# Pooled attention into a gated conv FFN: the depthwise conv of two and a half sequences moved from TensorE to ScalarE and VectorE, late pooling moved to GpSimd

## The chip, the cores and the metric

One NeuronCore of a Trainium2 chip runs the whole kernel in one launch. The metric is the device time of one execution in microseconds (us); lower is better. A difference of about 0.5% (1.1 us here) is what a measurement of this kernel can tell from no change.

## The reference

```
# attention, per sequence b (8) and head h (8), S = 576, D = 64
k_p, v_p = mean of k, v over 8 neighbouring positions     # 72 positions
attn = softmax(q @ k_p.T / 8)                             # 576 x 72
x[b] = concat over heads of attn @ v_p                    # 576 x 512
# gated FFN
h    = relu(x @ w_in)                                     # 576 x 1024
conv = w[0]*h[s-1] + w[1]*h[s] + w[2]*h[s+1]              # per channel, along the sequence
out  = (h * sigmoid(conv)) @ w_out                        # 576 x 512
```

q, k, v and the output are float32 in device memory; inside the kernel all operands of TensorE are bf16.

## The kernel before

**Sequences and groups.** The eight sequences are handled in four groups of two (0,1), (2,3), (4,5), (6,7). The order in which sequences reach the FFN is 0, 1, 3, 2, 4, 5, 6, 7. The attention of a group is cut into nine or ten row tiles of up to 128 rows; the FFN of a sequence into eight blocks `fb` of 128 of the 1024 channels; the output of a group into nine row tiles.

**Loads.** GpSimd (POOL) issues all loads of q, k, v and of the two weight matrices (L260 to L296), and they are converted to bf16 on the way. Keys of sequences 2 to 7 come in pairs into the only `kk` buffer (L267); v has three buffers (L278, L281).

**Pooling.** Keys of a pair are summed over 8 positions by three halving adds, `pool_pair` (L411: 2304, 1152, 576 elements for each partition), v by three halving adds and a masked product, `prep_v` (L457: 1280, 640, 320 elements; L461: 960). All of these run on VectorE (DVE). The keys are turned by TensorE (PE) into `kT` (L417, L440).

**Attention of a row tile.** Scores (PE, L553 or L566), row maximum (DVE, L579), subtraction of it (DVE L591, or for group 0 PE L599), exp (ScalarE, ACT, L617), a turn of the result (PE L628 with a copy L642, or from group 2 on a DMA, L637), the product with the pooled v (PE, L653), division by the row sum (DVE, L666 and L668), and a turn into `xT` (PE L685 and copy L693, or a DMA, L677).

**FFN of a sequence.** For each `fb`, two halves of `ffn_in` (PE, L698, four matmuls of 288 columns each; for sequence 0 by row tiles, L719) and a relu into `hT` (ACT, L707). The conv runs on PE as products with diagonal matrices `dw`. Sequences 0 to 3 do it in 64x64 tiles of the array (`ffn_conv`, L832), sequences 4 to 7 in 32x32 tiles (`ffn_conv16`, L790): one set of 48 matmuls covers four `fb` (an index `f4`, 0 or 1) and half a sequence, so a sequence takes four sets. `hT` has 64 more columns at each end; for sequences 4 to 7 GpSimd fills these by two copies for each `f4` (`ffn_wrap`, L780 and L781), so that a shifted tap is one plain slice. ACT takes tanh of the conv out of PSUM (L800, L843), DVE makes the gate from it: add 1 (L815, L854, L857: `tensor_scalar`, bf16, SBUF to SBUF) and multiply with `hT` (L819, L861: `tensor_tensor`, both operands in SBUF). Since 32x32 tiles leave their results on other partitions than they belong on, `ffn_gate16` adds 1 in five or six pieces of 32 to 128 partitions for each pair of `fb`.

**Output.** `ffn_out` (PE, L869, eight matmuls of 512 columns for a row tile, in two halves `j`), a copy of PSUM into `osb` (DVE or ACT, L880), and the store from SP or ACT (L892).

**Order.** Nothing is scheduled at run time. `Graph.ORDER` lists every operation of the kernel by number, with the engine where there is a choice, `FORMS` and `PLACES` give the tile modes and the buffers, and every engine works its own part of that list strictly in order, waiting on semaphores. The costs in the `add(...)` calls were used by a planner that is no longer in the file.

Of the kernel before, what the change touches and what calls it, by code (L numbers as in the profile page):

```python
# [33 lines left out]
class Graph:  # L34
# [23 lines left out]
    Q_DMA = (3,)  # L58
    SHIFT_DVE = 1
# [52 lines left out]
    )  # L112
    FORMS = (
        0, 1, 0, 0, 1, 1, 1, 1, 1, 0, 0, 0, 0, 1, 0, 0, 0, 0, 0, 0, 1, 1, 1, 0, 0, 0, 1, 0, 1, 0, 0, 0, 1, 0, 1, 1, 0, 0, 0, 0,
    )
    PLACES = (
# [51 lines left out]
def kernel(  # L168
# [759 lines left out]
    def nudge(kind, b):  # L928
        return 0.0
# [367 lines left out]
```

## Time and profile before

| | |
|---|---|
| median of 3 runs | 227.65 us (226.90 to 228.12) |
| the profiled execution, its own time | 227.96 us |
| the span of its profile | 226.2 us |
| mean granted TensorE clock | 0.992 |

The span runs from the first to the last instruction of the program; 1.76 us of the execution's own time lie around it. In the profile PE is a matmul, DVE VectorE, ACT ScalarE, POOL GpSimd, SP SyncE. A matmul's duration includes its way through the array, and matmuls overlap: 512 columns are shown with 374 ns, but they start 216 ns apart. How much room PE has is therefore read from start to start, not from the busy share. In what follows a stage is named by the sequence whose `ffn_in` begins it; in the trace of before these begin at 59.05 (sequence 1), 77.91 (3), 107.77 (2), 122.24 (4), 141.24 (5), 166.59 (6) and 184.75 us (7).

### The profile page before, as it was taken

The numbers are of one execution on the slowest core, as the hardware profiler recorded it, in microseconds if no ns is written. First come the engines' busy times: TensorE is split into PE (matmuls) and PEld (weight loads), VectorE is DVE, ScalarE is ACT, GpSimd is POOL, SyncE is SP. The second block draws the span as 40 slices with busy tenths as digits, with TensorE's granted clock in tenths as the row PEclk, the third lists the DMA queues.
The fourth block names the chain that finished last, engine by engine and source line by source line (L and its number), as shares of the span: only waits on it lengthen the run. The fifth ranks groups of instructions, "written<-read, shape, count | busy, mean of one in ns | idle before, by whom it ended". The sixth has DMA issues, their size and how long they took to land.

```text
span 226.2 us, 8092 instructions
## 1 busy us (share of the span) xinstructions
PE 210.7 (93%) x3469; PEld 143.9 (64%) x3469; DVE 189.5 (84%) x410; ACT 142.0 (63%) x239; POOL 35.8 (16%) x65
## 2 busy tenths in 40 slices
PE   7587999969999999999999999999998999999991
PEld 3556699855788777665787844666466646644451
DVE  7588877999999999989999998899984896859631
ACT  2057657999998878685679734783644746564220
POOL 7944231023220120000000010012001310110000
PEclk9799999999999999999999999999999999999999
DMA  5999999999999899864664574676567445021585
GB/s 85 177 191 207 207 207 207 207 207 206 208 208 206 128 192 128 194 149 84 156 127 99 113 120 104 139 153 108 71 129 168 99 51 139 3 51 35 142 200 183
DMA packets 48840, 32.72 MB, mean 145 GB/s; under 512 B 28300, under 2 KB 44324, under 8 KB 48804
## 3 DMA queue, kind: packets, MB, share of 16 engines
q0 software_dynamic: 16288, 16.26, 44.2%
q1 hardware_dynamic: 31716, 14.77, 32.4%
q10 hardware_dynamic: 800, 1.18, 1.6%
q8 instruction: 27, 0.44, 0.8%
q14 instruction: 9, 0.07, 0.1%
HBM read 32.52 MB, written 9.44 MB: 185 GB/s over the span
## 4 chain that ended last, share of the span: by engine, by line
PE 68%; DVE 19%; issue 5%; ACT 4%; DMA 1%; DVEq 0%; ACTq 0%
PE psum L869 25%; PE psum L698 18%; PE psum L653 5%; PE psum L790 4%; PE psum L719 4%; PE psum L832 4%; DVE negm L579 3%; DVE sd L591 2%; ACT tg L843 2%; PE psum L566 2%; PE psum L628 2%; DVE gT L857 2%; DVE x L668 2%; DVE gT L815 1%; DVE gT L861 1%
## 5 line engine op out<-in xcount | busy, mean ns | idle before, releaser
L869 PE MATMUL psum<-w_out_sb,gT 128*128 128x512 bf16 (+1 forms) x296 | 69.4, 374 | 0.5 <-DVE gT L861 0.5
L698 PE MATMUL psum<-xT,w_in_sb 128*128 128x288 bf16 x448 | 63.3, 286 | 0.8 <-DVE sd L591 0.5
L698 PEld LDWEIGHTS <-w_in_sb 128*128 128x128 bf16 x448 | 41.8, 98 | 14.4 <-issue 1.9
L707 ACT ACTIVATE hT<-psum 128x576 bf16<-128x576 f32 x56 | 35.1, 651 | 23.4 <-PE psum L698 21.0
L869 PEld LDWEIGHTS <-gT 128*128 128x128 bf16 x296 | 26.8, 98 | 26.5 <-DVE gT L861 0.7
L815 DVE TENSOR_SCALAR gT<-tg 32x576 bf16<-32x576 bf16 (+2 forms) x88 | 27.0, 307 | 7.1 <-ACT tg L800 5.9
L579 DVE TENSOR_REDUCE negm<-psum 128x8 f32<-128x576 f32 (+2 forms) x37 | 27.6, 752 | 2.9 <-PE psum L566 1.6
L668 DVE TENSOR_TENSOR x<-psum,r 128x512 bf16<-128x512 f32 (+1 forms) x37 | 25.6, 691 | 1.3
L800 ACT ACTIVATE tg<-psum 128x576 bf16<-128x576 f32 x32 | 19.4, 648 | 8.6 <-PE psum L790 5.6
L880 ACT COPY osb<-psum 128x512 f32<-128x512 f32 x21 | 12.2, 590 | 14.9 <-PE psum L869 10.5
L843 ACT ACTIVATE tg<-psum 128x576 bf16<-128x576 f32 x32 | 19.5, 652 | 2.6 <-PE psum L832 1.9
L617 ACT ACTIVATE e<-sd 128x576 bf16<-128x576 f32 x27 | 18.4, 685 | 4.2 <-DVE sd L591 4.2
L591 DVE TENSOR_TENSOR sd<-psum,negm 128x576 f32<-128x576 f32 x27 | 20.2, 754 | 0.8
L780 POOL COPY hT<-hT 128x252 bf16<-128x252 bf16 x8 | 3.5, 438 | 108.4 <-ACT hT L707 108.4
L653 PE MATMUL psum<-vm,eT 128*128 128x65 bf16 (+5 forms) x240 | 18.5, 221 | 1.6 <-DMA eT<-e 1.0
L653 PEld LDWEIGHTS <-eT 128*128 128x128 bf16 (+1 forms) x240 | 15.1, 101 | 5.2 <-DMA eT<-e 1.2
L832 PE MATMUL psum<-hT,dw 64*64 64x288 bf16 (+2 forms) x512 | 15.8, 256 | 0.5 <-ACT hT L707 0.2
L880 DVE COPY osb<-psum 128x512 f32<-128x512 f32 (+1 forms) x16 | 10.5, 653 | 6.8 <-PE psum L869 6.7
L832 PEld LDWEIGHTS <-dw 64*64 64x64 bf16 x512 | 12.6, 107 | 3.7 <-issue 2.7
L457 DVE TENSOR_TENSOR v<-v 128x1280 bf16<-128x1280 bf16 (+2 forms) x24 | 13.0, 542 | 1.3 <-DMA v<-in_v_dram 1.2
L819 DVE TENSOR_TENSOR gT<-gT,hT 128x1152 bf16<-128x1152 bf16 x16 | 12.5, 778 | 0.6
L642 ACT COPY eT<-psum 128x640 bf16<-128x640 bf16 (+1 forms) x17 | 11.1, 666 | 2.9 <-PE psum L628 2.8
(83 smaller groups left out, 254.7 us busy)
## 6 DMA issues: line engine op xcount, KB each, us to landing
out_dram<-osb SPq DMA_DIRECT2D x62, 128.0 KB, 2.4
v<-in_v_dram POOLq DMA_DIRECT2D x8, 512.0 KB, 16.2
qp<-in_q_dram POOLq DMA_DIRECT2D x7, 576.0 KB, 13.8
kk<-in_k_dram POOLq DMA_DIRECT2D x3, 1152.0 KB, 16.9
w_in_sb<-in_moe_w_in_dram POOLq DMA_DIRECT2D x2, 512.0 KB, 16.9
w_out_sb<-in_moe_w_out_dram POOLq DMA_DIRECT2D x1, 1024.0 KB, 24.5
out_dram<-osb ACTq DMA_DIRECT2D x8, 128.0 KB, 3.0
kk<-in_k_dram POOLq DMA_DIRECT2D x2, 288.0 KB, 5.0
```

Of the source, the lines that this page charges most:

```text
L579: nc.vector.tensor_reduce(out=a["m"][0:rows], in_=a["s"][0:rows, :, 0:2 * KW].rearrange("p a (h s) -> p a h s", s=Sp), axis=AX.X, op=OP.ma ...
L591: nc.vector.tensor_tensor(out=a["d"][0:rows], in0=a["s"][0:rows, :, 0:2 * KW].rearrange("p a (h s) -> p a h s", s=Sp), in1=a["m"][0:rows]. ...
L653: nc.tensor.matmul(out=a["o"][lo:hi, h // 4, (h % 4) * (D + 1):(h % 4 + x1 - x0) * (D + 1)], lhsT=a["eT"][:, j, lo:hi], rhs=buf("vm", b)[: ...
L668: nc.vector.tensor_tensor(out=a["x"][0:rows].rearrange("p (a h d) -> p a h d", a=2, d=D), in0=ov[:, :, :, 0:D], in1=r[0:rows].unsqueeze(3) ...
L698: nc.tensor.matmul(out=banks(ps)[:, j, 0:SC], lhsT=w_in_block(dc, fb), rhs=buf("xT", g)[:, dc, i * S + j * SC:i * S + (j + 1) * SC], start ...
L707: nc.scalar.activation(out=h_of(b)[:, fb].rearrange("p (a s) -> p a s", a=2), in_=banks(ps)[:, :, 0:SC], func=ACT.Relu, scale=0.5,)
L800: nc.scalar.activation(out=buf("tg", b, f4, h)[:, :, j * SC:(j + 1) * SC], in_=banks(ps)[:, :, 0:SC], func=ACT.Tanh, scale=0.5,)
L815: nc.vector.tensor_scalar(out=gate[lo:lo + n, 4 * f4 + s], in0=tg[src:src + n, x], scalar1=1.0, scalar2=None, op0=OP.add)
L832: nc.tensor.matmul(out=banks(pss[r ^ c])[c * D:(c + 1) * D, j, lo:hi], lhsT=dw[r * D:(r + 1) * D, tap * n_fb + fb, :], rhs=hT[r * D:(r + 1 ...
L843: nc.scalar.activation(out=tg.rearrange("p (a s) -> p a s", a=2), in_=banks(ps)[:, :, 0:SC], func=ACT.Tanh, scale=0.5,)
L869: nc.tensor.matmul(out=bank(ps)[0:rows, columns], lhsT=buf("gT", g)[:, fb, t * P:t * P + rows], rhs=w_out_sb[:, fb, columns], start=(fb == 0),
L880: copy(out=osb[0:rows, columns], in_=bank(ps)[0:rows, columns])
```

## The change

- **Taps.** For both halves `f4` of sequences 5 and 6 and for `f4` 0 of sequence 7 the conv is no longer done by PE. For each `fb`: ACT writes `w[1]*h` in float32 (Identity, with the weight as a scale for each partition), DVE adds the two other taps (`scalar_tensor_tensor`, 576 elements, bf16 and float32 in, float32 out), ACT takes tanh of that and writes it straight into `gT`. For each `f4`, DVE then adds 1 and multiplies by `hT` in two instructions of 2304 elements.
- **Pooling.** `prep_v` of sequences 3 to 7 and `pool_pair` of groups 2 and 3 run on GpSimd.
- **`ffn_conv`** reads `hT` with its offset, and its shorter runs stand in another order; its columns are the same. `ffn_in` of a half waits only for the attention tiles of that half.
- **Order.** ORDER, FORMS and PLACES are written out anew for all engines. In the new list DVE takes 6 instead of 16 of the output copies, 6 instead of 2 of the `eT` copies, 6 instead of 3 of the `xT` copies and 7 instead of 5 of the `qT` copies; ACT takes the others.

```diff
+    WRAP = (4, 5, 6, 7)
+    TAPS = ((5, 0), (5, 1), (6, 0), (6, 1), (7, 0))
+    V_POOL = (3, 4, 5, 6, 7)
+    K_POOL = (2, 3)
...
     def pool_pair(g, step):
         t, half = buf("kk", g), POOL * D >> step + 1
-        nc.vector.tensor_tensor(out=t[:, :, 0:half], in0=t[:, :, 0:half], in1=t[:, :, half:2 * half], op=OP.add)
+        engine = nc.gpsimd if g in Graph.K_POOL else nc.vector
+        engine.tensor_tensor(out=t[:, :, 0:half], in0=t[:, :, 0:half], in1=t[:, :, half:2 * half], op=OP.add)
...
     def prep_v(b, step):
+        engine = nc.gpsimd if b in Graph.V_POOL else nc.vector
...
-    def conv_todo():
+    def conv_todo(wrapped):
+        if wrapped:
+            return [[(tap, 0, SC, tap * TB + j * SC) for tap in (1, 0, 2)] for j in range(2)]
...
-                todo[j].append((tap, lo - j * SC, hi - j * SC, src))
-        return todo
+                todo[j].append((tap, lo - j * SC, hi - j * SC, TB + src))
+        return [[t[0]] + sorted(t[1:], key=lambda x: (x[2] - x[1]) % SC) for t in todo]
...
+    def ffn_tap(b, fb, tap):
+        acc, w = buf("tg", b, fb // 4, "tap", fb), convw[:, tap * n_fb + fb:tap * n_fb + fb + 1]
+        acc = acc.rearrange("p a s -> p (a s)").bitcast(FP32)
+        h = buf("hT", b)[:, fb, tap * TB:tap * TB + S]
+        if tap == 1:
+            nc.scalar.activation(out=acc, in_=h, func=ACT.Identity, scale=w)
+        else:
+            nc.vector.scalar_tensor_tensor(out=acc, in0=h, scalar=w, in1=acc, op0=OP.mult, op1=OP.add)
+
+    def ffn_tap_tanh(b, fb):
...
+        nc.scalar.activation(out=buf("gT", g)[:, fb, i * S:(i + 1) * S], in_=acc, func=ACT.Tanh, scale=0.5)
+
+    def ffn_tap_gate(b, f4):
...
+        nc.vector.tensor_scalar(out=gate, in0=gate, scalar1=1.0, scalar2=None, op0=OP.add)
+        nc.vector.tensor_tensor(out=gate, in0=gate, in1=h_of(b)[:, four], op=OP.mult)
...
-            prev = add(dve(d), key + nudge("kk", g) + Graph.KPOOL + step, lambda step=step: pool_pair(g, step),
+            prev = add({"POOL": 0.1 + (5.0, 2.5, 1.25)[step]} if g in Graph.K_POOL else dve(d), key + nudge("kk", g) + Graph.KPOOL + step, lambda step=step: pool_pair(g, step),
...
-            prev = add(dve(d), key + step * gap, lambda step=step: prep_v(b, step),
+            prev = add({"POOL": 0.1 + (2.8, 1.4, 0.7, 2.1)[step]} if b in Graph.V_POOL else dve(d), key + step * gap, lambda step=step: prep_v(b, step),
...
+    def half_of(b, j):
+        g, i = where[b]
+        ts = (0, 1, 2, 3, 4) if i == 0 else (9 if g in Graph.APART else 4, 5, 6, 7, 8)
+        return [xdone[g, t] for t in (ts[2:] if j else ts[:3])]
...
-                            after=need + [win[fb // 4], o], uses=[big, xtok[g], htok[b]], mode=FULL, count=8)
+                            after=half_of(b, j) + [win[fb // 4], o], uses=[big, xtok[g], htok[b]], mode=FULL, count=8)
...
+        for f4 in range(n_fb // 4):
+            if (b, f4) not in Graph.TAPS:
+                continue
+            tanh = []
+            for fb in range(4 * f4, 4 * f4 + 4):
+                tg, o = token("tg", b, f4, "tap", fb), None
+                for tap in (1, 0, 2):
+                    o = add(act(0.667) if tap == 1 else dve(0.757), w, lambda fb=fb, tap=tap: ffn_tap(b, fb, tap),
+                            after=[wraps[f4], dw0, o], uses=[tg, htok[b]])
+                tanh.append(add(act(0.667), w, lambda fb=fb: ffn_tap_tanh(b, fb), after=[o], uses=[tg, gtok[g]]))
+            gated = add(dve(0.75, 1.36), w, lambda f4=f4: ffn_tap_gate(b, f4), after=tanh, uses=[htok[b], gtok[g]])
+            gdone.setdefault(b, []).append(gated)
         for f4 in range(n_fb // 4 if b in Graph.SIXTEEN else 0):
+            if (b, f4) in Graph.TAPS:
+                continue
```

More of the change, by code (lines that the diff above doesn't have):

```diff
@@ L62 @@
     ORDER = (
[49 rows of a table removed]
[51 rows of a table added]
     )
     FORMS = (
-        0, 1, 0, 0, 1, 1, 1, 1, 1, 0, 0, 0, 0, 1, 0, 0, 0, 0, 0, 0, 1, 1, 1, 0, 0, 0, 1, 0, 1, 0, 0, 0, 1, 0, 1, 1, 0, 0, 0, 0,
+        0, 1, 0, 0, 1, 1, 1, 1, 1, 0, 0, 0, 0, 1, 0, 0, 0, 0, 0, 0, 0, 1, 1, 0, 0, 0, 0, 0, 0, 0, 0, 1, 1, 1, 1, 1, 0, 0, 1, 0,
     )
     PLACES = (
[18 rows of a table removed]
[17 rows of a table added]
     )
@@ L456, in prep_v @@
             half = POOL * D >> step + 1
-            nc.vector.tensor_tensor(
+            engine.tensor_tensor(
                 out=vt[:, :, 0:half], in0=vt[:, :, 0:half], in1=vt[:, :, half:2 * half], op=OP.add
@@ L460, in prep_v @@
             return
-        nc.vector.tensor_tensor(
+        engine.tensor_tensor(
             out=buf("vm", b)[:, :, :, 0:D],
@@ L819, in ffn_gate16 @@
         nc.vector.tensor_tensor(out=gate[:, both], in0=gate[:, both], in1=h_of(b)[:, both], op=OP.mult)
+    def ffn_tap(b, fb, tap):
[8 more added lines that the diff above has]
+        g, i = where[b]
+        acc = buf("tg", b, fb // 4, "tap", fb).rearrange("p a s -> p (a s)").bitcast(FP32)
+        nc.scalar.activation(out=buf("gT", g)[:, fb, i * S:(i + 1) * S], in_=acc, func=ACT.Tanh, scale=0.5)
+    def ffn_tap_gate(b, f4):
+        g, i = where[b]
+        four = slice(4 * f4, 4 * f4 + 4)
+        gate = buf("gT", g)[:, four, i * S:(i + 1) * S]
+        nc.vector.tensor_scalar(out=gate, in0=gate, scalar1=1.0, scalar2=None, op0=OP.add)
+        nc.vector.tensor_tensor(out=gate, in0=gate, in1=h_of(b)[:, four], op=OP.mult)
     def ffn_conv(b, f2, pss):
-        hT, todo = h_of(b), conv_todo()
+        hT, todo = buf("hT", b), conv_todo(b in Graph.WRAP)
         for turn in range(2):
@@ L1154 @@
     hdone, gdone, htok, gtok = {}, {}, {}, {}
+    def half_of(b, j):
+        g, i = where[b]
+        ts = (0, 1, 2, 3, 4) if i == 0 else (9 if g in Graph.APART else 4, 5, 6, 7, 8)
+        return [xdone[g, t] for t in (ts[2:] if j else ts[:3])]
     def add_ffn(b, w):
@@ L1161, in add_ffn @@
             gtok[g] = token("gT", g)
-        need = [xdone[g, t] for t in (range(5) if i == 0 else range(5, 10) if g in Graph.APART else range(4, 9))]
         relu = {}
@@ L1181, in add_ffn @@
                     o = add(pe(*[SC] * 4), w + 3 * fb + nudge("i", 8 * b + fb), lambda fb=fb, j=j, big=big: ffn_in(b, fb, j, big),
-                            after=need + [win[fb // 4], o], uses=[big, xtok[g], htok[b]], mode=FULL, count=8)
+                            after=half_of(b, j) + [win[fb // 4], o], uses=[big, xtok[g], htok[b]], mode=FULL, count=8)
                 relu[fb] = [add(act(0.65), w + 3 * fb + nudge("i", 8 * b + fb), lambda fb=fb, big=big: ffn_relu(b, fb, big), after=[o],
                                 uses=[big, htok[b]])]
+        wraps = [add({"POOL": 0.8}, w, lambda f4=f4: ffn_wrap(b, f4), uses=[htok[b]],
+                     after=[o for fb in range(4 * f4, 4 * f4 + 4) for o in relu[fb]] + [ends])
+                 for f4 in range(n_fb // 4 if b in Graph.WRAP else 0)]
+        for f4 in range(n_fb // 4):
[10 more added lines that the diff above has]
+            gdone.setdefault(b, []).append(gated)
         for f4 in range(n_fb // 4 if b in Graph.SIXTEEN else 0):
+            if (b, f4) in Graph.TAPS:
+                continue
             tgs = [token("tg", b, f4, h) for h in range(2)]
             tanh = [[], []]
-            wrap = add({"POOL": 0.8}, w, lambda f4=f4: ffn_wrap(b, f4), uses=[htok[b]],
-                       after=[o for fb in range(4 * f4, 4 * f4 + 4) for o in relu[fb]] + [ends])
+            wrap = wraps[f4]
             for j in range(2):
@@ L1202, in add_ffn @@
             fbs = (2 * f2, 2 * f2 + 1)
+            if (b, f2 // 2) in Graph.TAPS:
+                continue
             cbs, tg = [token("ps", n=2) for _ in fbs], token("tg", b, f2 // 2, f2 % 2)
-            conv = add({"PE": 0.75}, w + 6 * f2 + Graph.QCONV + nudge("c", 4 * b + f2), lambda f2=f2, cbs=cbs: ffn_conv(b, f2, cbs),
-                       after=relu[fbs[0]] + relu[fbs[1]] + dwo, uses=cbs + [tg, htok[b], gtok[g]], mode=QUARTER, count=64)
+            conv = add({"PE": 0.64 if b in Graph.WRAP else 0.66}, w + 6 * f2 + Graph.QCONV + nudge("c", 4 * b + f2), lambda f2=f2, cbs=cbs: ffn_conv(b, f2, cbs),
+                       after=(wraps[f2 // 2:f2 // 2 + 1] or relu[fbs[0]] + relu[fbs[1]]) + dwo, uses=cbs + [tg, htok[b], gtok[g]],
+                       mode=QUARTER, count=48 if b in Graph.WRAP else 64)
             for fb, cb in zip(fbs, cbs):
```

135 rows, old and new, of tables (ORDER, PLACES) are left out of this document.

## The prediction, on record before the changed kernel ran

> **What bounds the kernel now.** I read the page first, then the busy time by stage (the stretch of the trace that each sequence's `ffn_in` begins), then single conv sets in the timeline. The page's share of busy time and its chain of what ended last:
>
> ```profile
> PE 210.7 (93%) x3469; PEld 143.9 (64%) x3469; DVE 189.5 (84%) x410; ACT 142.0 (63%) x239; POOL 35.8 (16%) x65
> PE 68%; DVE 19%; issue 5%; ACT 4%; DMA 1%; DVEq 0%; ACTq 0%
> ```
>
> The chain lies two thirds on PE and one fifth on DVE. The stages tell why DVE is there at all (columns: stretch, its length, then the busy time of each engine):
>
> ```profile
> core 0: us, PE busy (x) PEld busy (x) DVE busy (x) ACT busy (x) POOL busy (x), PEclk, DMA share, GB/s
> 59.05:77.91 18.86, 18.71 (x325) 15.12 (x324) 18.45 (x38) 17.47 (x34) 3.64 (x5) 1.00 1.13 186
> 77.91:107.77 29.86, 29.25 (x455) 19.91 (x447) 28.33 (x55) 22.01 (x38) 1.33 (x2) 1.00 0.83 149
> 141.24:166.59 25.35, 25.03 (x443) 15.60 (x442) 23.73 (x55) 15.39 (x27) 2.00 (x4) 1.00 0.63 117
> 166.59:184.75 18.16, 17.12 (x299) 11.00 (x298) 13.70 (x34) 10.32 (x18) 3.50 (x6) 1.00 0.64 123
> 184.75:226.20 41.45, 36.80 (x472) 20.02 (x472) 24.76 (x61) 16.51 (x28) 1.66 (x4) 1.00 0.39 103
> ```
>
> From 59 to 108 us PE and DVE are both full: DVE is busy 46.8 of 48.7 us. From 141 us on PE alone is full; DVE idles 1.6, 4.5 and 16.7 us in the three last stages, ACT 10.0, 7.8 and 24.9. GpSimd is nearly empty everywhere. So the change takes from PE where PE binds, gives to DVE and ACT where they have room, and takes pooling from DVE where DVE is as full as PE.
>
> **Term 1: PE loses ten conv sets.** Two lines of the timeline (start, length, what):
>
> ```profile
> 182.99 0.73 PE L790 MATMUL psum<-hT,dw 32*32 32x288 bf16 x48
> 183.65 1.04 PE L869 MATMUL psum<-w_out_sb,gT 128*128 128x512 bf16 x4
> ```
>
> A set holds PE for 183.65 - 182.99 = 0.66 us, the change of tile mode included. Sixteen sets become six: 10 x 0.66 = **-6.6 us**. Six of these go from the stages of sequences 4 to 6, four from the last. The matmuls of `ffn_conv` (sequences 0 to 3) keep their columns and change places only; I cost that, and the finer waits of `ffn_in` (each half on its own tiles, in a fixed order), at nothing. The loads at the head stand in another order too (the first half of `w_in` before q of sequence 2); as the same bytes come, also nothing, with 1.5 us to either side.
>
> **Term 2: what DVE and ACT take on at the end.** The groups by form (count | busy, mean ns | idle before):
>
> ```profile
> L815 DVE TENSOR_SCALAR gT<-tg 32x576 bf16<-32x576 bf16 x64 | 19.5, 304 | 0.9
> L815 DVE TENSOR_SCALAR gT<-tg 128x576 bf16<-128x576 bf16 x8 | 2.6, 328 | 2.6 <-ACT tg L800 2.6
> L819 DVE TENSOR_TENSOR gT<-gT,hT 128x1152 bf16<-128x1152 bf16 x16 | 12.5, 778 | 0.6
> L591 DVE TENSOR_TENSOR sd<-psum,negm 128x576 f32<-128x576 f32 x27 | 20.2, 754 | 0.8
> L411 DVE TENSOR_TENSOR kk<-kk 128x2304 bf16<-128x2304 bf16 x3 | 4.1, 1352 | 0.8 <-DMA qp<-in_q_dram 0.8
> L617 ACT ACTIVATE e<-sd 128x576 bf16<-128x576 f32 x27 | 18.4, 685 | 4.2 <-DVE sd L591 4.2
> L800 ACT ACTIVATE tg<-psum 128x576 bf16<-128x576 f32 x32 | 19.4, 648 | 8.6 <-PE psum L790 5.6
> L880 ACT COPY osb<-psum 128x512 f32<-128x512 f32 x21 | 12.2, 590 | 14.9 <-PE psum L869 10.5
> L880 DVE COPY osb<-psum 128x512 f32<-128x512 f32 x14 | 9.6, 686 | 6.2 <-PE psum L869 6.1
> ```
>
> For each of the five `f4`, DVE gives up eleven pieces of add 1 (304 ns) and two products (778): 4.9 us. It takes eight taps of 576 float32 elements; none is in the trace, the nearest row is L591 with 754 ns, the bounds are the bf16 add 1 of as many elements (0.33) and the 2304-element product (1.35). I take 0.754: 6.0 us. It takes one add 1 of 2304 elements (between 0.33 and four times that, 1.31; I take 0.8) and a product of 2304 (1.35 by L411). Together 8.2 - 4.9 = 3.3, five times: +16.3 us. Ten output copies leave it, -6.9. Net +9.4 us against 22.8 us of idle time, of which the time after the last gate (40 matmuls of 216 ns, about 9 us) doesn't count. ACT takes 20 first taps and 20 tanh from SBUF (685 each by L617, bounds 590 and 1.35 us) for 20 of L800, plus ten copies: 27.4 - 13.0 + 5.9 = +20.3 us into 42.7 us of idle time. Both fit, but in the middle stage (sequence 6) three engines are then full, and each tap is a round ACT, DVE, DVE, ACT with three `tg` buffers for it. After the last `ffn_in` the new order gives PE 16 half output tiles and two sets, 15 us, and DVE eight taps, a copy and three gates, 13.7 us, before five output tiles that need the last gate. I charge **+1.6 us**, a quarter of term 1; the bounds are 0 (the idle time takes all) and 6.6 (the taps set the end and nothing is won).
>
> *On ACT, "ScalarE: Activation LUTs" of the Trainium skill (What ACT_TABLE_LOAD costs) says that an operand read for each partition through a pointer adds about 93 ns to an ACTIVATE; no row here has such a scale. By it the 20 first taps would cost 1.9 us more on ACT, and the sum would be at most that much later.*
>
> **Term 3: pooling on GpSimd, and who waits for it.** In the two stages that PE and DVE fill, DVE is freed of these (L457, L411 and L461 in that stretch, each in its own answer; below them two copies that it takes):
>
> ```profile
> 59.05:107.77 48.72, 4.85 (x9) 1.00 0.95 163
> 59.05:107.77 48.72, 5.10 (x6) 1.00 0.95 163
> 59.05:107.77 48.72, 1.94 (x3) 1.00 0.95 163
> ...
> L642 DVE COPY eT<-psum 128x640 bf16<-128x640 bf16 x2 | 1.0, 488 | 0.4 <-PE psum L628 0.4
> L693 DVE COPY xT<-psum 128x512 bf16<-128x512 bf16 x2 | 0.8, 416 | 0.0
> ```
>
> That is 11.9 us. The new list gives DVE 3 `eT` copies, 5 `xT` copies and 2 output copies more in these stages, 1.5 + 2.1 + 1.4 = 4.9 us, so it has 46.8 - 11.9 + 4.9 = 39.8 us to do in 48.7: **8.9 us of slack**.
>
> What GpSimd does to DVE meanwhile is visible in before, at the small copies of `ffn_wrap`:
>
> ```profile
> 198.56 0.40 POOL L780 COPY hT<-hT 128x252 bf16<-128x252 bf16 x1 [3.75 <-ACT hT L707]
> 155.36 0.40 POOL L780 COPY hT<-hT 128x252 bf16<-128x252 bf16 x1 [6.85 <-ACT hT L707]
> 155.44 0.93 DVE L819 TENSOR_TENSOR gT<-gT,hT 128x1152 bf16<-128x1152 bf16 x1
> 155.70 0.93 POOL L781 COPY hT<-hT 128x252 bf16<-128x252 bf16 x1
> 193.84 0.30 DVE L815 TENSOR_SCALAR gT<-tg 32x576 bf16<-32x576 bf16 x1
> 193.89 0.51 POOL L780 COPY hT<-hT 128x252 bf16<-128x252 bf16 x1 [11.99 <-ACT hT L707]
> 194.15 0.41 DVE L815 TENSOR_SCALAR gT<-tg 32x576 bf16<-32x576 bf16 x1
> 194.35 0.47 POOL L781 COPY hT<-hT 128x252 bf16<-128x252 bf16 x1
> 194.57 0.40 DVE L815 TENSOR_SCALAR gT<-tg 32x576 bf16<-32x576 bf16 x1
> L304 POOL TENSOR_SCALAR_AFFINE_SELECT gT<-gT x2: 781/799/817, 5.7 to 6.5; 64x648 bf16<-64x648 bf16 x2
> ```
>
> A copy alone takes 0.40 us. At 155.4 the gate's product started while a copy ran and took 0.93 instead of 0.78; the next copy, started 0.26 us into that product, ended just after it, at 156.6. At 193.8 the two engines go strictly in turn, and each instruction is longer by what the other had left. So a gate's instructions and a GpSimd instruction on SBUF exclude each other, whole instruction by whole instruction. So far the partner took 0.4 us; now it takes microseconds.
>
> *"SBUF — State Buffer" of the Trainium skill (Who interferes with whom) has this as a rule: VectorE in a two-port mode or with two SBUF inputs and GpSimd share a port pair under an exclusive lock for a whole instruction. By that rule the trace agrees.*
>
> Price of a GpSimd instruction: the copy (252 elements, 0.40) and the select of L304 (648, 0.80) give 1.0 ns for each element and 0.15 us for one input. No row has two inputs; bounds are 1.0 ns (inputs read together) and 3.2 (twice the copy's whole 1.58 ns). I take twice the slope, 2.0 ns: `prep_v` 2.7, 1.4, 0.8, 2.1 us (7.0), `pool_pair` 4.75, 2.45, 1.3 (8.5).
>
> *"GPSIMD Engine Reference" of the Trainium skill (3.1) gives 2.6 cycles at 1.2 GHz for an element of a two-input operation, 2.17 ns; by that figure the stall below would be about 8% larger, some 1.3 us.*
>
> In the two stages the new list has 17 such instructions (three steps of sequence 3, sequences 4 and 5, both pairs): 35.3 us of 48.7, a share of 0.72. DVE has 13 gates there, seven of one port instruction (add 1) and six of three (two adds, a product). A first instruction meets a running GpSimd one with that share, and then waits for its rest, the sum of squares over twice the sum, 96/70.6 = 1.36 us: 13 x 0.72 x 1.36 = 12.7 us. Each of the twelve that follow inside a gate can let in one whole GpSimd instruction, 2.08 us on average: at most 12 x 0.72 x 2.08 = 18.0. As a longer stage thins GpSimd's share (0.60), and as GpSimd often waits for a landing or for a pair's single `kk` buffer, I take 10.6 of the first and a third of the second, 5.4: **16 us of stall on DVE**, bounds 5 (priced at 1.0 ns, first instructions alone) and 31. Behind a stalled gate stand the row maxima, subtractions and divisions of the attention, and PE waits for these. Less the slack: 16 - 8.9 = **+7.1 us**. DVE's row maxima, subtractions and divisions read PSUM and go untouched.
>
> GpSimd's queue is in order, and loads now stand behind pooling: the load of pair 3 behind pair 2's three adds, v of sequence 5 behind the first add of sequence 4, v of 6 and 7 behind parts of pair 3. Before, such loads waited too:
>
> ```profile
> POOL v L278 <- DVE vm L461: 16.5, 3, 7.2
> POOL kk L267 <- DVE negm L579: 7.8, 1, 7.8
> ```
>
> so I charge nothing for the loads; if the gates hold GpSimd up in turn (25 instructions, 7 x 0.33 + 12 x 0.30 + 6 x 0.78 = 10.6 us), the keys of pair 3 come late for their turn at the start of sequence 2, some us of PE that the upper bound holds.
>
> **Sum.** 227.96 (the profiled execution's own time) - 6.6 + 1.6 + 7.1 = 230.1 us. That execution was 0.31 us above the median, so **229.8 us** on the median's scale.
>
> **Rivals.** (1) *Not slower: the stalls fit into DVE's slack.* Place: the two stages from 59 to 108 us; it decides below 8.9 us of stall, for instance if GpSimd's adds cost 1.0 ns an element. Then 227.65 - 6.6 + 1.6 = 222.6 us; with the taps hidden too, 221.0. For it: 8.9 us is half of what I expect, and GpSimd idles while it waits for landings. Against it: the strict turns at 193.8. (2) *The port decides fully*: 31 us of stall, 227.65 - 5.0 + 22.1 = 244.8; halfway there, 237. For it: gates and pooling together want 10.6 + 35.3 = 46 of the port's 48.7 us. Against: GpSimd must be ready at each gate. (3) *They cancel*: stalls of 13 to 15 us, or taps that end last without stalls, both 227 to 228.7. That the change doesn't do what it says is hardly possible: the new list has 288 matmuls of L790's kind for 768.
>
> **How the numbers follow.** Forecast 0.45 (226.5 to 238 is its own range), rival 1 0.33, rival 2 0.12, rival 3 0.10. Slower by over 0.5% (about what a measurement of this kernel can tell from no change): 0.57; within: 0.10; faster: 0.33. The range must reach into rival 1 and half into rival 2: 221.5 to 239.0 leaves out the best of the one and the worst of the other.
>
> **What would show it.** Term 1: conv sets 16 to 6, PE's stages of sequences 5 and 7 shorter. Term 2: taps near 0.75 us, no DVE or ACT wait that ends in the last gate. Term 3: GpSimd adds of 2 to 5 us, and DVE's add-1 and product groups with means far above 304 to 328 and 778 ns between 59 and 115 us; the sum of that excess is the stall. If those means stay within 0.3 us of before, term 3 is wrong and rival 1 holds.

## The result and the profile after

The changed kernel takes **255.3 us** (median of 4 runs, 253.82 to 257.65) beside 227.4 us for the kernel before on the same chip (226.9 to 228.12): a ratio of 1.120, 95% interval 1.116 to 1.124. Here and below a median is of all runs, while a ratio leaves out runs that took over 1.5% longer than the fastest of their kernel (here the one of 257.65 us). That is slower, as forecast, but the loss is 27.9 us where the forecast had 2 and the top of the range 11. The profiled execution has a span of 252.7 us. Its page begins like this (busy time of each engine, then the chain that ended last):

```profile
PE 209.8 (83%) x2993; PEld 142.6 (56%) x2993; DVE 213.4 (84%) x368; ACT 154.7 (61%) x260; POOL 92.2 (36%) x91
...
PE 40%; DVE 34%; DMA 10%; issue 8%; POOL 4%; ACT 2%; DVEq 0%; ACTq 0%; POOLq 0%
```

DVE is busy 24 us longer than before, although it has been relieved of pooling, and its part of the chain rises from 19 to 34%. The busy time by stage (start and end, length, busy time of each engine, granted clock):

```profile
core 0: us, PE busy (x) PEld busy (x) DVE busy (x) ACT busy (x) POOL busy (x), PEclk, DMA share, GB/s
0.00:64.46 64.46, 50.91 (x972) 38.28 (x972) 54.20 (x114) 38.68 (x63) 29.30 (x45) 1.00 1.15 187
64.46:83.53 19.07, 18.74 (x305) 15.70 (x306) 16.39 (x32) 15.13 (x27) 10.71 (x6) 1.00 0.49 75
83.53:133.89 50.36, 33.64 (x452) 22.18 (x450) 44.30 (x51) 19.39 (x34) 27.90 (x18) 0.80 0.70 119
133.89:148.31 14.42, 14.26 (x285) 11.21 (x285) 13.52 (x29) 10.29 (x19) 0.00 (x0) 1.00 0.42 89
148.31:173.15 24.84, 20.26 (x321) 12.81 (x319) 19.96 (x39) 13.62 (x23) 11.62 (x9) 1.00 0.66 100
173.15:192.89 19.74, 19.12 (x258) 12.31 (x259) 17.72 (x38) 15.31 (x26) 3.36 (x6) 1.00 0.60 116
192.89:210.10 17.21, 16.49 (x121) 10.86 (x121) 17.00 (x26) 15.58 (x28) 3.53 (x3) 1.00 0.49 103
210.10:252.70 42.60, 36.35 (x289) 19.23 (x287) 30.29 (x46) 26.69 (x46) 5.81 (x6) 0.97 0.48 124
```

Against before, the head is 5.4 us longer (59.05 to 64.46), the stage of sequence 1 as long (18.86 to 19.07), that of **sequence 3 longer by 20.5** (29.86 to 50.36), that of 4 by 5.8 (19.00 to 24.84); those of 5 and 6 are shorter by 5.6 and 0.95, the last longer by 1.15. The stages of 4 and 5 are best read together: the one has 70 matmuls more than before (251 to 321), the other 185 less (443 to 258), and only 96 of these are conv sets that are gone from the two. Work has moved across their border, and the two together are as long as before (44.35 to 44.58). The stage of 3 alone holds three quarters of the loss. GpSimd is busy for 27.9 us in it, where it had 1.33.

The groups by form tell what changed there (count | busy, mean ns | idle before):

```profile
L837 DVE SCALAR_TENSOR_TENSOR tg<-hT,convw,tg 128x576 f32<-128x576 bf16 x40 | 31.0, 823 | 0.2
L887 DVE TENSOR_SCALAR gT<-tg 64x576 bf16<-64x576 bf16 x32 | 20.9, 654 | 0.6
L891 DVE TENSOR_TENSOR gT<-gT,hT 128x1152 bf16<-128x1152 bf16 x16 | 15.6, 978 | 0.6
L835 ACT ACTIVATE tg<-hT,convw 128x576 f32<-128x576 bf16 x20 | 15.1, 771 | 0.1
L842 ACT ACTIVATE gT<-tg 128x576 bf16<-128x576 f32 x20 | 13.2, 684 | 4.0 <-DVE tg L837 4.0
L464 POOL TENSOR_TENSOR v<-v 128x1280 bf16<-128x1280 bf16 x5 | 13.1, 2620 | 5.9 <-DMA v<-in_v_dram 5.9
L884 DVE TENSOR_SCALAR gT<-tg 128x576 bf16<-128x576 bf16 x16 | 11.3, 712 | 1.3 <-ACT tg L873 1.3
L417 POOL TENSOR_TENSOR kk<-kk 128x2304 bf16<-128x2304 bf16 x2 | 9.1, 4540 | 0.6 <-DMA kk<-in_k_dram 0.6
```

The gate's three groups (L884, L887, L891; L854, L857, L861 before) were 5.0, 9.9 and 12.1 us; they are 11.3, 20.9 and 15.6, 20.8 us more for the same instructions. The lines of GpSimd and DVE in the timeline from 81.7 to 88.3 us show how one add 1 of 0.31 us comes to last 3.5 us (start, length, engine, line; x2 is two instructions in one line):

```profile
81.72 1.01 POOL L272 DMA_DIRECT2D kk<-in_k_dram  x1 [8.14 <-PE psum L692]
82.05 6.19 DVE L887 TENSOR_SCALAR gT<-tg 64x576 bf16<-64x576 bf16 x2
82.74 2.62 POOL L464 TENSOR_TENSOR v<-v 128x1280 bf16<-128x1280 bf16 x1
85.30 0.79 POOL L283 DMA_DIRECT2D v<-in_v_dram  x1
86.08 0.56 POOL L286 DMA_DIRECT2D v<-in_v_dram  x1
86.66 2.26 POOL L464 TENSOR_TENSOR v<-v 128x640 bf16<-128x640 bf16 x2
88.27 1.27 DVE L891 TENSOR_TENSOR gT<-gT,hT 128x1152 bf16<-128x1152 bf16 x1
```

The first add 1 starts during the issue of a load, has not run when that issue ends, and then waits for the whole 2.62 us add of v; it ends just after it, at 85.5. The second meets the two issues of the next load and the first of the two adds behind them, and ends at 88.2. Two instructions of 0.31 us have taken 6.19.

### The profile page after: what moved, and what is told of

Read it like the earlier page. It is cut to its first block, busy times and chain, and to the rows that moved or that the text cites. A ratio compares the mean times of both kernels' runs of the same rounds, so it can differ in the third digit from the quotient of the medians.

```text
span 252.7 us, 7119 instructions
## 1 busy us (share of the span) xinstructions
PE 209.8 (83%) x2993; PEld 142.6 (56%) x2993; DVE 213.4 (84%) x368; ACT 154.7 (61%) x260; POOL 92.2 (36%) x91
## 4 chain that ended last, share of the span: by engine, by line
PE 40%; DVE 34%; DMA 10%; issue 8%; POOL 4%; ACT 2%; DVEq 0%; ACTq 0%; POOLq 0%
PE psum L705 13%; PE psum L899 12%; DVE tg L837 8%; DMA qp<-in_q_dram 7%; DVE gT L887 6%; DVE negm L586 4%; DVE sd L598 3%; PE psum L726 3%; DMA xT<-x 3%; PE psum L660 3%; PE psum L862 3%; DVE gT L891 2%; DVE gT L884 2%; DVE x L675 2%; DVE v L464 1%
## 5 line engine op out<-in xcount | busy, mean ns | idle before, releaser
L705 PE MATMUL psum<-xT,w_in_sb 128*128 128x288 bf16 x448 | 66.4, 295 | 13.8 <-DVE sd L598 7.7
L789 POOL COPY hT<-hT 128x252 bf16<-128x252 bf16 x8 | 6.7, 843 | 90.0 <-ACT hT L714 69.9
L837 DVE SCALAR_TENSOR_TENSOR tg<-hT,convw,tg 128x576 f32<-128x576 bf16 x40 | 31.0, 823 | 0.2
L873 ACT ACTIVATE tg<-psum 128x576 bf16<-128x576 f32 x32 | 19.2, 650 | 18.3 <-issue 12.9
L464 POOL TENSOR_TENSOR v<-v 128x1280 bf16<-128x1280 bf16 (+2 forms) x15 | 24.2, 1610 | 6.5 <-DMA v<-in_v_dram 5.9
L910 ACT COPY osb<-psum 128x512 f32<-128x512 f32 (+1 forms) x31 | 17.4, 579 | 11.9 <-PE psum L899 10.1
L887 DVE TENSOR_SCALAR gT<-tg 64x576 bf16<-64x576 bf16 x32 | 20.9, 654 | 0.6
L624 ACT ACTIVATE e<-sd 128x576 bf16<-128x576 f32 x27 | 18.1, 682 | 3.7 <-DVE sd L598 3.7
L417 POOL TENSOR_TENSOR kk<-kk 128x2304 bf16<-128x2304 bf16 (+2 forms) x6 | 16.5, 2754 | 0.7 <-DMA kk<-in_k_dram 0.6
L891 DVE TENSOR_TENSOR gT<-gT,hT 128x1152 bf16<-128x1152 bf16 x16 | 15.6, 978 | 0.6
L842 ACT ACTIVATE gT<-tg 128x576 bf16<-128x576 f32 x20 | 13.2, 684 | 4.0 <-DVE tg L837 4.0
```

The source lines that it names most:

```text
L464: engine.tensor_tensor(out=vt[:, :, 0:half], in0=vt[:, :, 0:half], in1=vt[:, :, half:2 * half], op=OP.add)
L705: nc.tensor.matmul(out=banks(ps)[:, j, 0:SC], lhsT=w_in_block(dc, fb), rhs=buf("xT", g)[:, dc, i * S + j * SC:i * S + (j + 1) * SC], start ...
L837: nc.vector.scalar_tensor_tensor(out=acc, in0=h, scalar=w, in1=acc, op0=OP.mult, op1=OP.add)
L887: nc.vector.tensor_scalar(out=gate[r * D:(r + 1) * D, fb], in0=tg[(1 - r) * D:(2 - r) * D], scalar1=1.0, scalar2=None, op0=OP.add)
L891: nc.vector.tensor_tensor(out=gate[:, both], in0=gate[:, both], in1=h_of(b)[:, both], op=OP.mult)
```

## The experiments

**One part undone.** Pooling went back to VectorE in whole or in part; order and taps stayed.

```diff
-    V_POOL = (3, 4, 5, 6, 7)
-    K_POOL = (2, 3)
+    V_POOL = ()              # a_nopool, a_nopool2, a_konly
+    K_POOL = ()              # a_nopool, a_nopool2, a_vonly
```

> The changed kernel with all pooling (v of sequences 3 to 7, key pairs 2 and 3) back on VectorE; the new order and the tap convs stay. Theory A (pooling on GpSimd and VectorE's gate instructions shut each other out, and that is nearly the whole loss): the 20.6 us of stretched gates in the stage of sequence 3 and the 5.4 us at the head go, VectorE gets 16.5 us of pooling back (11.4 for v, 5.1 for pairs), some of it in full stages: 226 to 232 us, gate groups back to means of 0.31 and 0.78 us. Rival B (the new order and the taps cost the time, the pooling only happens to be there): 245 to 255 us. Rival C (GpSimd's late loads and late pooled keys and v): as A in total, but with the gates stretched no less where wraps run, and gaps on PE before attention gone.

Measured (a_nopool): 241.2 us, ratio 1.058 (1.052 to 1.064). 14 us came back, not 24 to 29: theory A as the whole story falls, and so do B and C, which forecast A's time.

> The changed kernel with the two key pairs pooled on VectorE again, v of sequences 3 to 7 still on GpSimd. Theory A: only the stretches against the pair adds go (three gates of the stage of sequence 3, 3.7, 2.8 and 1.7 us long, some 6 us with what follows), and VectorE gets 5.1 us more work: 247 to 252 us. Rival B: no change, 255 us. If the number of GpSimd instructions counts and not their length, less falls away: 252 to 256 us.

Measured (a_vonly): 256.5 us, 1.126 (1.119 to 1.132): no gain, which theory A did not expect.

> The changed kernel with v of sequences 3 to 7 prepared on VectorE again, key pairs 2 and 3 still pooled on GpSimd. Theory A: the head's 5.4 us and the stretches against v of sequences 4 to 6 go (some 12 us in the stage of sequence 3), VectorE gets 11.4 us of work back: 236 to 244 us. Rival B: 250 to 255 us.

Measured (a_konly): 254.6 us, 1.110 (1.099 to 1.121), no gain beyond the intervals, and again not theory A's 236 to 244. It lies in rival B's span, but the groups explain both misses without B. In a_vonly the gates are stretched by 14.7 us, v of sequence 2 (on DVE) by some 3, and DVE has 5.1 us of pooling back: 22.8 us. In a_konly the gates are stretched by 9.1, DVE's own v instructions by 4.7, and it has 11.4 us back: 25.2. In the changed kernel it is 20.8 + 3.5 + 0 = 24.3. DVE's burden is about the same in all three; half the pooling does not cost half.

**One part alone.** The kernel before, with its order and convs, and only the engine of the pooling changed.

```diff
-        nc.vector.tensor_tensor(out=t[:, :, 0:half], ...
+        engine = nc.gpsimd if g in Graph.K_POOL else nc.vector    # likewise in prep_v
+        engine.tensor_tensor(out=t[:, :, 0:half], ...
```

> The kernel before, with its own order and its convs on TensorE, where only the pooling of v of sequences 3 to 7 and of key pairs 2 and 3 runs on GpSimd. Theory A: the stall comes without the new order and without taps: 240 to 256 us, gate instructions of 1 to 3.7 us in the two full stages. Rival B: 222 to 229 us, since VectorE has 16.5 us less to do and nothing else moved. Rival C (late loads behind pooling): also slower, but with gate instructions of their old length and TensorE waiting for keys, v or their loads.

Measured (b_pool): 252.2 us, 1.109 (1.104 to 1.114). Theory A holds: pooling on GpSimd alone costs 25 us, without taps and without the new order. Its gates:

```profile
L865 DVE TENSOR_TENSOR gT<-gT,hT 128x1152 bf16<-128x1152 bf16 x16 | 19.6, 1225 | 0.6
L861 DVE TENSOR_SCALAR gT<-tg 64x576 bf16<-64x576 bf16 x32 | 16.3, 509 | 0.6
L858 DVE TENSOR_SCALAR gT<-tg 128x576 bf16<-128x576 bf16 x16 | 9.6, 605 | 1.1 <-ACT tg L847 1.0
```

They are 7.5 + 6.4 + 4.6 = 18.5 us longer than before, with the work unchanged. PE also waits here 4.7 us for v and 2.4 us for keys that GpSimd has pooled (0.5 us for v before), so a part of the 25 us may be rival C's late results.

**Length or place?** In b_pool the results also come later and GpSimd's queue is fuller. b_thin shortens GpSimd's adds at their places, which leaves most of the pooling out, and has the mask product of v (2.0 us each in b_pool) back on VectorE; b_dummy keeps all of the kernel before and puts GpSimd instructions beside it that nobody waits for.

```diff
+        w = half // 8                                  # b_thin, on GpSimd
-                out=vt[:, :, 0:half], in0=vt[:, :, 0:half], in1=vt[:, :, half:2 * half], op=OP.add
+                out=vt[:, :, 0:w], in0=vt[:, :, 0:w], in1=vt[:, :, half:half + w], op=OP.add
...
+            upper = vt[:, :, half:2 * half]            # b_dummy, behind VectorE's add
+            nc.gpsimd.tensor_tensor(out=upper, in0=upper, in1=upper, op=OP.add)
```

> The kernel before with the adds of the pooling (v of sequences 3 to 7, key pairs 2 and 3) on GpSimd at the same places as in b_pool (252.2 us), but each add over one eighth of its elements, so that most of the pooling is left out; the mask product of v stays on VectorE. Theory A (the length of the GpSimd instruction, for which VectorE's gates wait): 224 to 229 us. Rival Q (the place in GpSimd's queue and the waits between the engines cost the time, whatever the instruction's length): 238 to 252 us.

Measured (b_thin): 227.0 us, 0.9995 (0.997 to 1.002). Theory A: with short instructions at the same places nothing is lost. Nothing is won either, though DVE is busy for 179.7 us instead of 189.5. Its gates are back:

```profile
L867 DVE TENSOR_TENSOR gT<-gT,hT 128x1152 bf16<-128x1152 bf16 x16 | 12.3, 770 | 0.6
L863 DVE TENSOR_SCALAR gT<-tg 64x576 bf16<-64x576 bf16 x32 | 10.4, 325 | 0.6
```

> The kernel before, unchanged, with VectorE doing all its pooling, and beside each pooling instruction of v of sequences 3 to 7 and of key pairs 2 and 3 an idle instruction on GpSimd of the same shape, whose result nothing reads (it works in the upper half that the add has already used). Nothing is later than before but through GpSimd itself. Theory A (exclusion: VectorE's gates and its own adds wait for GpSimd instructions): 242 to 256 us. Rival (in b_pool the late results cost the time, not the exclusion): 226 to 231 us.

Measured (b_dummy): 254.8 us, 1.120 (1.115 to 1.125). Theory A: no VectorE or TensorE instruction waits for these GpSimd instructions by the program, and they cost 27 us. Only later loads stand behind them in GpSimd's queue, and those are not what is lost: DVE waits 0.4 us for a load of v (1.2 before), and PE for no load. Here DVE's own adds of v meet them, as well as its gates:

```profile
L872 DVE TENSOR_SCALAR gT<-tg 64x576 bf16<-64x576 bf16 x32 | 15.4, 480 | 0.6
L462 DVE TENSOR_TENSOR v<-v 128x1280 bf16<-128x1280 bf16 x8 | 9.8, 1225 | 0.4 <-DMA v<-in_v_dram 0.4
```

The add of 1280 took 816 ns before and takes 1225 here. The exclusion is shown from both sides: without length no loss, and a loss of the same size where no result is waited for.

**What the taps are worth, with the new order of the end.** The list of before up to the first `ffn_in` of sequence 4, behind it the new list.

```diff
+ORDER = before's list up to ffn_in(4), then the operations left, in the new list's order
+    V_POOL = ()              # h4_pool: (7,)
+    K_POOL = ()
```

> The list of the kernel before up to the first ffn_in of sequence 4, then the list of the changed kernel with its taps; all pooling on VectorE. It has the tap convs and the new order of the end, and neither pooling on GpSimd nor the new order of the first stages. Theory A (the taps and the end of the new order win, as the stages of sequences 5 to 7 of the changed kernel are 5.4 us shorter together; what costs time lies before): 220 to 224 us. Rival B (the taps cost time): 229 to 238 us.

Measured (h4_dve): 225.0 us, **0.990 (0.987 to 0.994)**, just above theory A's span; B falls. It is the fastest kernel of this study. Its last four stages:

```profile
core 0: us, PE busy (x) PEld busy (x) DVE busy (x) ACT busy (x) POOL busy (x), PEclk, DMA share, GB/s
121.68:143.18 21.50, 19.28 (x312) 12.41 (x313) 20.54 (x41) 12.72 (x23) 0.73 (x2) 1.00 0.60 111
143.18:163.45 20.27, 19.10 (x257) 12.48 (x259) 19.69 (x44) 15.85 (x27) 3.64 (x6) 1.00 0.54 112
163.45:180.65 17.20, 16.38 (x118) 10.86 (x120) 16.99 (x26) 15.57 (x28) 3.52 (x3) 1.00 0.45 96
180.65:223.30 42.65, 35.93 (x285) 19.21 (x287) 30.29 (x46) 26.71 (x46) 5.82 (x6) 0.98 0.48 124
```

Against before: +2.5, -5.1, -0.96 and +1.2 us, together -2.4. The first two, read together, are 2.6 us shorter, and DVE is busy 40.2 of their 41.8 us. The stages of 6 and 7 are those of the changed kernel to a tenth of a microsecond; in the stage of 6 DVE is busy 16.99 of 17.20 us.

> As h4_dve, with v of sequence 7 prepared on GpSimd (four instructions of 2.6, 1.4, 0.8 and 2.0 us in the stage of sequence 4, where VectorE's work reads PSUM mostly). Theory A (the port costs only where gate instructions and pooling meet): within 1.5 us of h4_dve, either way. If any pooling on GpSimd costs VectorE its whole length: 5 to 7 us slower than h4_dve.

Measured (h4_pool): 225.8 us, 0.994 (0.992 to 0.997), 0.8 us above h4_dve: theory A. The four GpSimd instructions, 7.1 us, meet one short add of v (0.79 us instead of 0.32) and one mask product (1.04 instead of 0.65) of DVE and no gate (whose group means are 0.31, 0.32 and 0.76 us); they cost next to nothing, and win nothing.

**What the new order is worth.** The complement of h4_dve, and a second profile of a_nopool.

```diff
+ORDER = the new list up to ffn_in(4), then the operations left, in before's order   # p4_dve
+    TAPS = ()
+    V_POOL = ()
+    K_POOL = ()
```

> The complement: the list of the changed kernel up to the first ffn_in of sequence 4, then the list of the kernel before with its convs on TensorE; no taps, all pooling on VectorE. Theory A (the new order of the first stages, which gives VectorE 4.9 us more copies and counts on its pooling being gone, overfills VectorE): 238 to 246 us, the same stages long as in the changed kernel with pooling on VectorE. Rival B (the order is harmless, the taps cost): 226 to 230 us.

Measured (p4_dve): 241.0 us, 1.062 (1.057 to 1.068). Theory A in its size: the order of the first stages costs 14 us without taps and without pooling on GpSimd.

> The changed kernel with all pooling on VectorE once more, for a profile at the granted clock of the others (the first one was 0.757): 241 us; Theory A: its stages up to sequence 4 are longer than before's by some 18 us in sum, the later ones shorter by some 5; rival B: the stages of sequences 5 to 7 are the longer ones.

Measured (a_nopool2): 241.9 us, with stages longer by 2.8 (head), 2.3 (1), 7.0 (3), 0.3 (2) and 5.8 (4), 18.1 in sum, and shorter by 4.1 behind that: theory A.

**Why the order costs.** Two candidates: loads that come late, and copies that overfill DVE.

```diff
 prep_v(2, step 3)
+load_v(5)                    # n_loads, a_loads, a_thin_loads: forward in ORDER
...
 prep_v(3, step 3)
+load_v(6)
...
-att_copy on VectorE, 5 times; att_copy_out, 5 times; ffn_copy, 2 times; copy_q; copy_keys
+the same on ScalarE, and 5 others the other way     # n_copies, on top of n_loads
```

> The changed kernel's list with its taps and all pooling on VectorE (241.2 us as it stood), and the loads of v of sequences 5 and 6 moved forward in the list: that of 5 to right behind the preparing of v of sequence 2, that of 6 to behind that of sequence 3, about where the kernel before has them. Theory L (the new list puts these loads behind the load of key pair 3, which waits 26 us for its buffer; the transfers stand still from 73 to 81 us and then run beside the attention's own small transfers, one of which took 7.6 us): 225 to 231 us. Rival O (the new list gives VectorE more copies than it has room for): 237 to 242 us.

Measured (n_loads): 238.1 us, 1.050 (1.045 to 1.055). 3 us at most; theory L falls as the main cause.

> As n_loads (238.1 us), with the PSUM copies of the first stages (19 of them; 14 on VectorE in the new list) given to the engine that does them in the kernel before, at the places of the new list. Theory O (VectorE is overfull in the stages of sequences 1 and 3 by those copies): 231 to 235 us. Rival (the order itself, not the share of the copies): 237 to 239 us.

Measured (n_copies): 237.6 us, 1.043 (1.039 to 1.048). The rival: nine copies fewer on DVE change nothing beyond the intervals. (The new list gives DVE seven `xT` copies, not six as the section on the change has it; here it is three, as before.)

> The changed kernel whole, pooling on GpSimd, with the same two loads moved forward, so that they stand ahead of the pooling in GpSimd's queue. Theory L with the port (two causes that add): the late transfers go, the stretched gates stay: 240 to 248 us. Rival (the stretched gates set the time of those stages and the loads wait in their shadow): 252 to 256 us.

Measured (a_loads): 257.4 us, 1.134 (1.131 to 1.137): the rival, if anything worse. The late loads are not what the changed kernel suffers from.

**The new list with short pooling.** As b_thin, in the changed kernel, with the mask product of v on VectorE.

```diff
+            w = half // 8 if b in Graph.V_POOL else half    # a_thin; likewise for the pairs
-                out=vt[:, :, 0:half], in0=vt[:, :, 0:half], in1=vt[:, :, half:2 * half], op=OP.add
+                out=vt[:, :, 0:w], in0=vt[:, :, 0:w], in1=vt[:, :, half:half + w], op=OP.add
```

> The changed kernel with its list, taps and engines, but each of GpSimd's pooling adds over one eighth of its elements (most of that pooling left out) and the mask product of v on VectorE, as in b_thin. Theory A (exclusion by GpSimd is the whole loss; the list fits a VectorE without pooling): 221 to 227 us. Rival O (the list's order itself costs what n_loads showed): 234 to 240 us.

Measured (a_thin): 236.0 us, 1.039 (1.036 to 1.042), rival O's size. 19.3 of the 27.9 us go with the length of GpSimd's adds and with its mask products, 8.6 stay with the new list, taps included. Three of its stages (sequences 1, 3 and 4):

```profile
61.01:80.88 19.87, 18.79 (x306) 15.78 (x306) 17.14 (x35) 15.99 (x29) 4.33 (x7) 1.00 0.66 109
80.88:114.06 33.18, 29.33 (x447) 19.83 (x451) 26.42 (x51) 19.20 (x33) 7.88 (x15) 0.95 0.98 165
128.47:154.84 26.37, 21.58 (x318) 13.51 (x319) 20.37 (x39) 13.53 (x23) 2.33 (x7) 0.94 0.54 95
```

The stage of sequence 3 is 33.18 us instead of 50.36. That of 4 is longer than before by 7.4 us even so (with the stage of 5, 46.1 us against 44.4), so its length in the changed kernel doesn't need GpSimd. On the chain of a_thin that stage is entered and left through a turn of the attention's output by DMA (start, length):

```profile
127.74 4.41 DMA xT<-x
...
150.66 4.13 DMA xT<-x
```

PE's `ffn_in` of sequences 4 and 5 stand behind these. The chain of the changed kernel has two of them as well, of 4.63 and 3.54 us. PE waits for such turns 3.7 us in a_thin, 4.4 in the changed kernel, and not at all in the kernel before and in h4_dve. They are not what the first stages lose: in p4_dve PE waits for them 0.2 us, and 14 us are lost all the same.

> As a_thin, with the loads of v of sequences 5 and 6 moved forward as in n_loads. Theory L (late loads cost time once nothing else hides them): 2 to 5 us below a_thin. Rival: within 1 us of it.

Measured (a_thin_loads): 238.1 us, 1.049 (1.045 to 1.053), 2.2 us above a_thin. Theory L falls here too.

**Attempts at a better end.** `h671` follows before's list to just ahead of `ffn_in(5)`; `h4_t56` and `h_end671` take the taps of sequence 7 out.

```diff
-    TAPS = ((5, 0), (5, 1), (6, 0), (6, 1), (7, 0))
+    TAPS = ((5, 0), (5, 1), (6, 0), (6, 1))                # h4_t56, h_end671
```

> As h4_dve (225.0 us), but the list of the kernel before is followed further, to just ahead of the first ffn_in of sequence 5, then that of the changed kernel. In h4_dve the stage of sequence 4 was 2.5 us longer than before, those of 5 to 7 5.0 us shorter. If the longer stage comes from the new order in it: 222 to 223.5 us. If the taps draw the work of that stage into the next anyway: 225 us.

Measured (h671): 226.3 us, 0.996 (0.994 to 0.999): above both expectations; the stage of sequence 4 became 22.3 us, not 19. The two lists do not join well there.

> As h4_dve (225.0 us), with the convs of sequence 7 all on TensorE: taps for sequences 5 and 6 alone. Theory A (the taps of sequence 7 stand between the last ffn_in and the last gates, where VectorE sets the end): 222.5 to 224.5 us. Rival (two conv sets on TensorE at 0.66 us cost what they did): 225.5 to 226.5 us.

Measured (h4_t56): 233.0 us, 1.026 (1.023 to 1.029): slower than both expectations.

> As h671, with the convs of sequence 7 on TensorE and the end in the order of the kernel before, the last taps of sequence 6 spread through it; taps for sequences 5 and 6 alone. If the taps of sequence 7 lengthen the end (its stage was 1.2 us longer in the changed kernel with two conv sets less): 1 to 2 us below h671. If spreading the taps makes TensorE wait for gates at the end: 1 to 4 us above it.

Measured (h_end671): 236.3 us, 1.040 (1.036 to 1.044), 10 us above h671 and again slower than both. In both the last stage is 51 us instead of 42.6: at the places where I put the conv sets PE waits, 3.0 us for a bank to be copied out in the one, 4.3 us for a relu and 3.3 us for tanh in the other. This tells of those places and not of the taps of sequence 7, which stay untested by themselves.

## Why the prediction was wrong

Two steps failed: the new order, costed at nothing, and the slack that was taken off the stall. The path before, h4_dve, a_thin, after splits the loss, if the parts add: taps and end -2.4 us (227.4 to 225.0), the order of the rest +11.0 (225.0 to 236.0), GpSimd's long adds and mask products +19.3 (236.0 to 255.3). The prediction had -5.0, 0 and +7.1. The parts do depend on each other: with all pooling on DVE the same order costs 16 us (a_nopool against h4_dve).

- **Terms 1 and 2** (-6.6 + 1.6): the mechanism was right, the size off by 2.6 us. The tap took 0.823 us (predicted 0.754), the 2304-element product 1.39 (1.35), its add 1 0.79 (0.8), ACT's first tap 0.771 and tanh 0.684 (0.685 each). In h4_dve the stages of 4 and 5 together gain 2.6 us and that of 6 gains 0.96; DVE is full there (40.2 of 41.8 and 17.0 of 17.2 us). In the last stage two sets less on PE end 1.2 us later. "Both fit" was true of the sums and not of the stages. L835 reads its weight through a pointer and takes 87 ns more than L842, which has none (and another function and other types); "ScalarE: Activation LUTs" of the Trainium skill (What ACT_TABLE_LOAD costs) has about 93 ns for this, and by it the trace agrees.
- **Edits at nothing**: "The matmuls of `ffn_conv` keep their columns and change places only; I cost that, and the finer waits ... at nothing", and the loads' order at 0 with 1.5 us to either side. This step failed, by 11 us. A new list is a change of its own. It was compared by counts of instructions for each engine; what each engine waits for in its new place was not. By stages, a_thin is longer than h4_dve by 2.5 us in the head, 1.0 in that of sequence 1, 3.3 in that of 3 and 4.3 in those of 4 and 5. Neither the loads of v that were moved nor the share of the copies is the main cause, by the runs. DMA turns ahead of `ffn_in` of 4 and 5 are seen in the chain, but not isolated. What in the new order costs the rest stays open.
- **Prices of term 3** were right: 2.62 us for 1280 elements (2.7 predicted), 4.54 for 2304 (4.75).
- **The stall.** That gates and GpSimd exclude each other was right. The stall was sized at 16 us with a bound of 31; it is 20.8 on the gates and 3.5 on DVE's own v of sequence 2 in the head, which the prediction left out. It also counted only GpSimd's arithmetic: its load issues of 0.5 to 1.0 us can hold an add 1 as well, and hand on to the next add. Two slips in its sum changed little: a third of 18.0 is 6.0 and not 5.4, and the lower bound of 5 us comes out as 3.6.
- **"Less the slack: 16 - 8.9 = +7.1"** is the step that failed most: the stall cost its whole length and more. The three groups in the stage of sequence 3 (length, then the group's busy time), each in its own answer, in the changed kernel:

```profile
83.53:133.89 50.36, 7.93 (x6) 0.80 0.70 119
83.53:133.89 50.36, 13.22 (x12) 0.80 0.70 119
83.53:133.89 50.36, 8.05 (x6) 0.80 0.70 119
```

and in a_thin:

```profile
80.88:114.06 33.18, 1.81 (x6) 0.95 0.98 165
80.88:114.06 33.18, 3.75 (x10) 0.95 0.98 165
80.88:114.06 33.18, 4.60 (x6) 0.95 0.98 165
```

29.2 us against 10.2, and with two more add 1 of 0.31 allowed for, 18.4 us of stretch in this stage. The stage is 17.2 us longer. DVE's idle time in it is 50.36 - 44.30 = 6.1 us with the stalls and 33.18 - 26.42 = 6.8 without: nearly no idle time was used up. Over the two stages that the prediction summed, DVE idles 9.5 us in a_thin, near the 8.9 credited, and still 8.7 in the changed kernel. The idle time consists of waits for PE's scores and products with v and for a tanh. When a gate stalls, the subtractions and all that follows them stall behind it, and PE too (the waits of PE in the changed kernel, us in total, times, longest, begin with 11.0 us at once for a subtraction). Slack worked out as a difference of sums was there on paper and could not be spent:

```profile
PE psum L862 <- DVE sd L598: 11.0, 1, 11.0
```

PE stands still for the whole of that wait. b_thin says the same from the other side: 9.8 us less busy time on DVE won nothing. That the whole difference of 19.3 us is this stall is not shown piece by piece; the stage of sequence 3 has 17.2 of it.

Of the rivals, the port deciding fully (244.8 us, 0.12) was the nearest, with the right mechanism; its price (31 us of stall less 8.9 of slack) still lacked the order. Rival 1, for which DVE's slack would have sufficed, got 0.33 by that slack. The test named for term 3 (means far above 304 to 328 and 778 ns) came out as written: 654, 712, 978 ns.

## What to carry to other kernels

An engine that looks empty is not free help: count what it shares with the engine it is to relieve, and put its work where the other has no instruction of the kind that excludes it, or keep its instructions short. Do not credit idle time that is a sum of small waits in an in-order chain against long stalls. When an order is written out anew, test it apart from the change it was written for: here the taps with the new end win 1%, and the rest of the list and the move lose 13%.

## What the runs showed of the hardware

GpSimd's load issues can hold up DVE's add 1, and with one exception they did not hold up its two-input operations. The trace of the kernel before had it already, in three places (start, length; only the lines of the two instructions):

```profile
46.54 0.76 POOL L260 DMA_DIRECT2D qp<-in_q_dram  x1 [4.83 <-DMA w_out_sb<-in_moe_w_out_dram]
46.66 0.76 DVE L861 TENSOR_TENSOR gT<-gT,hT 128x1152 bf16<-128x1152 bf16 x1
...
49.35 0.74 POOL L260 DMA_DIRECT2D qp<-in_q_dram  x1 [2.06 <-DMA qp<-in_q_dram]
49.46 0.30 DVE L857 TENSOR_SCALAR gT<-tg 64x576 bf16<-64x576 bf16 x1
...
81.61 0.77 POOL L278 DMA_DIRECT2D v<-in_v_dram  x1 [5.67 <-DVE vm L461]
81.89 0.60 DVE L854 TENSOR_SCALAR gT<-tg 128x576 bf16<-128x576 bf16 x1
```

The product that runs beside most of the issue at 46.54 takes its 0.76 us. The add 1 at 81.89, begun 0.28 us into an issue, takes 0.60 us instead of 0.32, to just behind the issue's end. The one at 49.46, begun 0.10 us into an issue, takes its 0.30, so an issue doesn't hold an add 1 over its whole length. "SBUF — State Buffer" of the Trainium skill (Who interferes with whom) has the same division between the two operations: `tensor_scalar` can enter a two-port mode and contends, while `tensor_tensor` contends only with GpSimd's reads. By it the trace agrees. The exception is in a_konly: at 104.51 a product beside four issues in a row, with no other instruction on GpSimd, took 1.71 us instead of 0.76, and no run shows why. The 0.3 us at 81.89 was harmless; with a long add queued right behind the issue it becomes the 3.5 us at 82.05.

In the stage of sequence 3 a stall of DVE also left PE slower for a while. Three stretches of the changed kernel behind the wait of 11.0 us, which ended at 114.87 (the clock is the third number from the end):

```profile
114.87:118.00 3.13, 3.13 (x52) 2.20 (x52) 1.42 (x3) 1.38 (x3) 0.00 (x0) 0.50 0.83 192
118.00:122.00 4.00, 4.00 (x30) 2.98 (x29) 2.62 (x7) 0.99 (x3) 0.00 (x0) 0.66 0.14 29
122.00:126.00 4.00, 4.00 (x109) 2.38 (x110) 2.60 (x6) 2.84 (x6) 0.00 (x0) 1.00 0.33 74
```

Over the whole stage the granted clock was 0.80 and PE was busy 33.64 us, in a_thin 0.95 and 29.33: 4.3 us more for about the same matmuls (452 and 447). How much of this lengthened the stage, which DVE set, no run shows.
